# Moving the first load of V's diagonal block to SyncE's queue, and two GpSimd steps to later rounds, in a causal attention + PReLU MLP kernel

## The chip, the cores and the metric

One NeuronCore of one Trainium2 chip runs the whole program. The metric is device time in microseconds (us) of one execution; lower is better. The engines are TensorE (PE), VectorE (DVE), ScalarE (ACT), GpSimd (POOL) and SyncE (SP). SP only issues DMAs here; ACT and POOL issue a few as well. Each engine runs its instructions strictly in the order in which they are written, and waits on semaphores for the others.

## The reference, cut to what matters

```python
# q, k, v: (4, 12, 448, 64) float32; w_in (768, 2048); w_out (2048, 768); alpha (2048,)
scores = q @ k.transpose(0, 1, 3, 2) / sqrt(64)
scores = where(upper triangle, -1e9, scores)
attn = softmax(scores)                     # with the row maximum taken off
x = (attn @ v).transpose(0, 2, 1, 3).reshape(1792, 768)
h = x @ w_in
g = maximum(h, 0) + alpha * minimum(h, 0)
return g @ w_out                           # (1792, 768)
```

## The kernel before

**Tiles.** Attention works on 24 pairs of heads, p = 0 to 23 (four batches, six pairs each). A row of 448 positions is cut into a first piece of 64 and three blocks of 128. For each pair the scores of block i are built in a PSUM bank (`scores`, L563 and L555), DVE masks them and takes the row maximum (`row_max`, L576), ACT takes the exponential and the row sums (`row_exp`, L591), DVE forms the reciprocals (`row_rec`, L604 and L605), POOL multiplies (`row_norm`, L534), PE transposes (`transpose_p`, L642; `transpose_halves`, L633), ACT or DVE copies the transposes out of PSUM (`pt_copy`, L530 on ACT, L532 on DVE), and PE multiplies by V (`av`, L661; `av_halves`, L669). The last of these, L669, reads the 64-row diagonal blocks of V from `vd`, four tiles used in turn (`vd[p % 4]`), which `load_vd` fills by two DMAs a pair (L504). POOL clears the four tiles once at the start (L495).

**MLP.** Both matrix products that follow (L408 and L1342) use a seven-product block scheme: sums and differences of blocks, each split into a rounded high part (`x1h`) and a remainder (`x1l`). While attention runs, spare slots on the engines already prepare its operands: `t_hi` rounds a block on POOL (the letter `h`, a TENSOR_SCALAR on L534 that writes `x1h`), `t_lo` takes the remainder on DVE (the letter `l`, L737), `t_four` forms a difference of two blocks on POOL (the digit `4`, L752), and the first weights are decoded from raw words by `A`, `I`, `C`, `D`, `G` and `+` (`+` is an integer addition on POOL, L331; `C` is a clamp on POOL, L315; `D` is a shift on DVE, L319) and by `S`, `sub`, `pcast` and `cast` (`sub` is L390 on POOL).

**What sets the order.** Attention is written round by round. In round n a string of step names with lags says what is emitted: `EX10+2` means the exponential of block 1, first head, of pair n - 2. `ORDER` is the string of most rounds; `ROUNDS` gives rounds 2 and 3, and the dictionary `first` gives changed strings to some rounds. Instructions are emitted in that order, so it is the order on each engine. Steps in short: `LK`, `LQ` load K and Q (lag 0), `S0`, `S1`, `S2` are scores, `MX` maxima, `EX` exponentials, `RC` reciprocals, `NO` the multiplications, `PT` and `PTH` transposes, `C10`, `C00`, `C20`, `C21`, `C30` the copies out of PSUM (`a` on ACT, `d` on DVE), `AV` and `AH` the products with V, `LW` is `load_vd`. The table `EARLY` says for each round which preparing steps are put into it: `l`, `D`, `G`, `S` run in the middle of the round ahead of the reciprocals, `h`, `4`, `+`, `sub`, `pcast`, `C` after the POOL multiplications of that round. On PE a round begins with `PTH`, `AV`, `AH` of pair n - 4, then `PT` of pair n - 3 (12 matmuls on L642), then scores of pair n - 1.

**Queues.** K, Q and most of V come through SP's queue, K of pairs 0 and 1 through ACT's and part of V through POOL's. `load_vd` uses ACT's queue for pair 0 and SP's for the others. For pair 0 it stands in round 1, behind `LQ+0`; that is ahead of the first exponentials in ACT's order.

Of the kernel before, what the change touches and what calls it, by code (L numbers as in the profile page):

```python
# [24 lines left out]
WARM = 8  # L25
EARLY = {
# [4 lines left out]
}  # L31
GAP = {25: "l", 26: "l"}
# [8 lines left out]
ORDER = """  # L41
# [2 lines left out]
ROUNDS = {2: """  # L44
LK+0 LQ+0 EX10+2 EX11+2 MX00+2 EX00+2 MX01+2 EX01+2 MX20+2 EX20+2 MX21+2 EX21+2 RA+2 NO10+2p NO11+2p NO00+2p NO01+2p MX30+2 S0+1 S1+1 PT1+2 PT0+2 MX10+1 MX11+1 EX30+2 RB+2 NO20+2p NO21+2d NO30+2p
""", 3: """
LK+0 LQ+0 EX10+2 EX11+2 MX00+2 EX00+2 MX01+2 EX01+2 MX20+2 S2+2 EX20+2 MX21+2 PT2+3 EX21+2 C00+3d C20+3a C21+3d C10+3d S0+1 S1+1 SF+1 LW+2 MX30+2 EX30+2 RC+2 NO10+2p NO11+2p NO00+2p NO01+2p NO20+2p NO21+2p NO30+2p MX10+1 MX11+1
"""}


# [143 lines left out]
def kernel(  # L194
# [10 lines left out]
    nc = tc.nc  # L205
    B, NPAIR, D, _, S = qt.shape
# [4 lines left out]
    LQ = S - NQ * QP  # L211
# [249 lines left out]
    T, vs, p3, masks, qd, vd = {}, [], [], [], [], []  # L461

    def half(j):
        return slice(j * D, (j + 1) * D)
# [32 lines left out]
    def load_vd(p):  # L497

        b, hp = pairs[p]
        for j in range(2):  # L500
            x = v[b, hp, :LQ, j]
            stride = x.ap[0][0]
            x = bass.AP(tensor=x.tensor, offset=x.offset, ap=[list(x.ap[0]), [(QP - CP) * stride + 2 * D, NQ + 1], list(x.ap[-1])])
            (nc.sync if p else nc.scalar).dma_start(out=vd[p % 4][half(j), :, j], in_=x)  # L504

    def load_v(b):
        for hs, n in ((hs, n) for hs in ((slice(0, NK), slice(NK, NPAIR)) if b == 0 else (slice(0, NPAIR),)) for n in range(NQ)):
# [242 lines left out]
    def t_four():  # L750
# [4 lines left out]
        "LV": load_v_next, "RC": row_rec, "RA": lambda p: row_rec(p, slice(0, 4)),  # L755
        "RB": lambda p: row_rec(p, slice(4, 2 * NQ + 1)), "AV": av, "AH": av_halves,
        "PTH": transpose_halves, "LW": load_vd, "BB": lambda p: None, "XH": x_hi, "XF": x_sums, "XL": x_lo,
        "ST": lambda p: flush(stores), "XN": lambda p: None, "LT": lambda p: None,
    }
# [25 lines left out]
    def order_of(text):  # L785
        order = []
        for w in text.split():
            name, lag = w.split("+")
            if name in choice:
                eng = {"a": nc.scalar, "d": nc.vector, "p": nc.gpsimd}[lag[-1]]  # L790
                order.append((int(lag[:-1]), name, lambda p, fn=choice[name], eng=eng: fn(p, eng)))
            else:
                order.append((int(lag), name, steps[name]))
        return order

    def attention(hooks):
        order, first = order_of(ORDER), {n: order_of(x) for n, x in ROUNDS.items()}

        for n in (5, 6, 7, 11, 12, 13, 20, 21, 22, 23):
            text = ORDER.replace("C00+3a", "C00+3d") if n in (5, 6, 11, 20, 22) else ORDER  # L800
            if n in (6, 7, 11, 12, 13, 21, 23):
                text = text.replace("C30+4a ", "").replace("MX20+2 ", "MX20+2 C30+4d ")
            first[n] = order_of(text)
        first[1], first[4] = order_of(ORDER.replace("LW+1 ", "").replace("LQ+0", "LQ+0 LW+1")), order_of(ORDER.replace("C00+3a", "C00+3d").replace("LW+1", "LW+2 LW+1"))

        text = ORDER.replace("C10+3a ", "").replace("EH+4 ", "EH+4 C10+3a ").replace("PT2+3 ", "PT2+3 PTH+3 ")
        first[26] = order_of(text.replace("C21+3d ", "C21+3d C30+3d "))
        first[27] = order_of(ORDER.replace("PTH+4 ", "").replace("C30+4a ", ""))
        last = max(lag for lag, *_ in order)
        for n in range(len(pairs) + last):  # L810
            for lag, name, fn in first.get(n, order):
                if 0 <= n - lag < len(pairs):
                    fn(n - lag)
                    for hook in hooks.get((n - lag, name), ()):
                        hook()
# [61 lines left out]
    def ready_bank():  # L877

        b = ring.popleft()
        nc.tensor.matmul(b[:, :S], wi[0, "A11"][:, 0, :P], x1h[:, 0, 0], start=True, stop=True, skip_group_check=True)  # L880
        return b
# [66 lines left out]
    with tc.manual_schedule():  # L948
# [15 lines left out]
        for t in masks:  # L964
# [5 lines left out]
            out=mk, in_=mk, pattern=[[-1, QP]], compare_op=ALU.is_ge, fill=NEG, base=0,  # L970
# [22 lines left out]
        after(last, "LT", scores_over)  # L993
        after(last, "AH", attention_over)
        attention(hooks)
        t13, t24 = (tf[:, 2 * i : 2 * i + 2].rearrange("p a k n -> p (a k n)") for i in range(2))
        rooms["t"], rooms["v"] = Slots([]), Slots([])
# [6 lines left out]
        v_, z, y, x = ring.popleft(), ready_bank(), ring.popleft(), ring.popleft()  # L1004
# [544 lines left out]
```

## Time and profile before

| What | Value |
|---|---|
| Three runs, median (lowest to highest) | 584.0 us (583.35 to 584.0) |
| The profiled execution: time, and span from first to last instruction | 583.36 us, 581.6 us |
| PE busy | 568.9 us, 98% |
| DVE busy | 471.4 us, 81% |
| ACT busy | 384.8 us, 66% |
| POOL busy | 290.1 us, 50% |
| Mean granted TensorE clock | 0.990 of full |
| Attention | from the start to about 175 us of the span |

The page divides the span into 40 slices of 14.5 us. PE is busy for nine tenths or more in nearly all of them; the first slice has six tenths. The row of the granted clock shows full speed everywhere but in the second slice, at six tenths. A busy PE is not a PE at its peak, so a stage is read by what its engines wait for and by the length of its rounds.

### The profile page before, as it was taken

To read this page: it belongs to the slowest core of one execution; us is meant where nothing else is said; L and a number is where in the kernel's file an instruction comes from. 1 tells how busy PE (TensorE), PEld (TensorE's weight loads), DVE (VectorE), ACT (ScalarE), POOL (GpSimd) and SP (SyncE) were. 2 spreads that over 40 slices of the span, in tenths; PEclk is the share of its full clock that TensorE was granted. 3 is DMA by queue.
4 is the path that set the end of the run, shared out by engine and by line. 5 is a ranking of instruction groups with operands and counts; after the bars stand their busy time and mean duration, and the time that the engine had idled before them with its cause. 6 is when DMAs were issued, how large, how long until landed. Compare 5 with 4: busy or idle time off the path is not lost.

```text
span 581.6 us, 11540 instructions
## 1 busy us (share of the span) xinstructions
PE 568.9 (98%) x3921; PEld 503.6 (87%) x3921; DVE 471.4 (81%) x989; ACT 384.8 (66%) x904; POOL 290.1 (50%) x338
## 2 busy tenths in 40 slices
PE   6999999999999999999999999999989999999997
PEld 3577767677788999999999999999989999999997
DVE  1789899999978886768777687888997899797763
ACT  2789888898858565655566655696765666665431
POOL 4666677797753444434454431436144543356420
PEclk9699999999999999999999999999999999999999
DMA  7565654854326675847677657593352414512532
GB/s 186 147 165 120 167 148 105 226 140 130 107 71 227 225 226 201 270 185 243 218 217 257 218 192 230 171 351 127 100 154 80 139 51 133 143 38 91 182 109 108
DMA packets 94074, 95.92 MB, mean 165 GB/s; under 512 B 24096, under 2 KB 83136, under 8 KB 94016
## 3 DMA queue, kind: packets, MB, share of 16 engines
q1 hardware_dynamic: 92624, 93.52, 52.6%
q0 software_dynamic: 528, 1.08, 0.8%
q10 hardware_dynamic: 864, 0.59, 0.4%
q8 instruction: 31, 0.51, 0.4%
q14 instruction: 27, 0.22, 0.1%
HBM read 66.85 MB, written 28.31 MB: 164 GB/s over the span
## 4 chain that ended last, share of the span: by engine, by line
PE 84%; DVE 9%; ACT 2%; DMA 2%; issue 1%; POOL 1%; ACTq 0%; SPq 0%; DVEq 0%; POOLq 0%
PE bank L408 36%; PE bank L1342 32%; PE bank L563 5%; PE bank L642 4%; PE bank L661 3%; DVE bank L576 2%; PE bank L633 2%; PE bank L669 1%; ACT p L591 1%; DVE tf L693 1%; POOL p L534 1%; DMA v<-in_v_dram 1%; DVE x1l L737 1%; DMA kr<-in_k_dram 1%; DVE ptf L532 1%
## 5 line engine op out<-in xcount | busy, mean ns | idle before, releaser
L534 POOL TENSOR_SCALAR p<-p,rs 128x320 f32<-128x320 f32 (+3 forms) x165 | 83.6, 526 | 45.0 <-DVE rs L605 24.5
L1342 PE MATMUL bank<-x1h,x1l 128*128 128x384 f32 x540 | 98.7, 335 | 1.0 <-DVE x1h L1279 0.9
L1342 PEld LDWEIGHTS bank<-x1h,x1l 128*128 128x128 f32 x540 | 94.3, 188 | 1.6 <-DVE x1h L1279 1.2
L591 ACT ACTIVATE p<-bank,nm 128x192 f32<-128x192 f32 (+3 forms) x168 | 81.6, 510 | 21.0 <-DVE nm L576 13.5
L576 DVE CUSTOM_DVE_ANT_0 bank<-bank,mask 128x192 f32<-128x192 f32 (+3 forms) x168 | 70.4, 483 | 12.1 <-PE bank L563 6.1
L432 ACT ACTIVATE tf<-bank 128x448 f32<-128x448 f32 x64 | 34.3, 541 | 40.1 <-PE bank L408 30.1
L563 PE MATMUL bank<-kr,qr 64*128 64x448 f32 (+2 forms) x288 | 55.5, 476 | 5.0 <-ACT p L591 4.7
L436 DVE SCALAR_TENSOR_TENSOR tf<-tf,om,bank 128x448 f32<-128x448 f32 x64 | 41.6, 674 | 6.4 <-ACT tf L432 6.0
L408 PE MATMUL bank<-x1h,wir 128*128 128x448 f32 x192 | 44.7, 368 | 0.0
L563 PEld LDWEIGHTS bank<-kr,qr 64*128 64x128 f32 x288 | 30.3, 198 | 16.4 <-ACT p L591 9.4
L1342 PE MATMUL bank<-x1h,gset 128*128 128x384 f32 x216 | 40.4, 338 | 0.9 <-DVE acc L1355 0.9
L1342 PEld LDWEIGHTS bank<-x1h,gset 128*128 128x128 f32 x216 | 37.9, 188 | 1.2 <-ACT acc L1476 1.2
L642 PE MATMUL bank<-ident,p 128*128 128x128 f32 x288 | 38.5, 284 | 0.3 <-POOL p L534 0.2
L408 PEld LDWEIGHTS bank<-x1h,wir 128*128 128x128 f32 x192 | 35.9, 188 | 3.4
L591 ACT ACTIVATION_READ_ACCUMULATOR p<-bank,nm 128x1 f32 x168 | 36.8, 219 | 0.0
L331 POOL TENSOR_TENSOR dec<-dec,tf 128x768 int32<-128x768 int32 x11 | 22.1, 2009 | 29.1 <-ACT tf L432 15.6
L1320 POOL TENSOR_TENSOR x1l<-acc,x1l 128x512 fp32r<-128x512 f32 x12 | 16.3, 1362 | 40.7 <-ACT x1l L1316 31.7
L530 ACT ACTIVATE ptf<-bank 128x256 f32<-128x256 f32 (+2 forms) x80 | 34.7, 501 | 2.9 <-PE bank L642 1.6
L422 DVE TENSOR_TENSOR bank<-bank,tf 128x448 f32<-128x448 f32 x30 | 18.9, 629 | 20.7 <-PE bank L408 19.4
L642 PEld LDWEIGHTS bank<-ident,p 128*128 128x128 f32 x288 | 31.9, 143 | 4.0 <-POOL p L534 2.2
L661 PE MATMUL bank<-ptf,v 128*64 128x128 f32 (+2 forms) x288 | 35.3, 380 | 0.0
L408 PE MATMUL bank<-x1h,wie 128*128 128x448 f32 x144 | 33.4, 367 | 0.0
(196 smaller groups left out, 1398.3 us busy)
## 6 DMA issues: line engine op xcount, KB each, us to landing
gd<-tf SPq DMA_DIRECT2D x64, 224.0 KB, 2.0
tf<-gd SPq DMA_DIRECT2D x28, 256.0 KB, 4.5
acc<-gd SPq DMA_DIRECT2D x28, 256.0 KB, 4.3
dec<-in_moe_w_in_dram SPq DMA_DIRECT2D x9, 768.0 KB, 5.2
tf<-in_moe_w_in_dram SPq DMA_DIRECT2D x7, 768.0 KB, 4.6
dec<-in_moe_w_out_dram SPq DMA_DIRECT2D x7, 768.0 KB, 4.9
tf<-in_moe_w_out_dram SPq DMA_DIRECT2D x7, 768.0 KB, 4.2
dec<-wd SPq DMA_DIRECT2D x13, 384.0 KB, 4.9
```

Of the source, the lines that this page charges most:

```text
L331: nc.gpsimd.tensor_tensor(out=y, in0=y, in1=low, op=ALU.add)
L408: nc.tensor.matmul(ps, w[:, u, k * P : (k + 1) * P], x[:, k], start=(st in ("P1", "P5") and i == 0), stop=(i == len(mms) - 1), skip_group_ ...
L432: nc.scalar.activation(t, bank_of(g, b, role), AF.Relu, scale=-1.0)
L436: stt(out=t, in0=t, scalar=om[:, f : f + 1], in1=bank_of(g, b, role), op0=ALU.mult, op1=ALU.add)
L530: eng.activation(out, x, AF.Copy, scale=side)
L534: eng.tensor_scalar(out=out, in0=x, scalar1=side, scalar2=1.0, op0=ALU.mult, op1=ALU.mult)
L563: nc.tensor.matmul(ps[:, o : o + lim], T["q", p][half(j), i * QP : (i + 1) * QP], T["k", p][half(j), :lim], start=(o == 0), stop=(n > 0 or ...
L576: nc.vector.tensor_tensor_reduce(out=t, in0=t, in1=mask_of(i), scale=-SCALE, scalar=MOST_F32, op0=ALU.add, op1=ALU.min, accum_out=nm,)
L591: nc.scalar.activation(T["p", p, i][:, j, : t.shape[1]], t, AF.Exp, scale=-1.0, bias=T.pop(("nm", p, i, j)), accum_out=T["sm", p][:, z : z ...
L642: nc.tensor.transpose(ps[:, j - js[0], c], t[:, j, c * QP : (c + 1) * QP], T["ident"])
L661: nc.tensor.matmul(out[half(j), c * QP + LQ :], vs[b % 2][:, hp, c, j], x[:, : (NQ - c) * QP], start=(c == 0), stop=False, skip_group_chec ...
L1342: nc.tensor.matmul(ps, x, w, start=(st in ("P1", "P5")[: 1 if Q else 2] and i == 0), stop=(i == len(mms) - 1), skip_group_check=True,)
```

## The change

There are three parts in the diff.

1. `load_vd` always issues on SP, and the load of pair 0 is written in round 3, as `LW+3` ahead of `LW+2`, no longer in round 1.
2. In `EARLY`, round 15 loses `4 h`, round 18 gets a `4`, round 24 gets an `h`. The steps come from iterators, so the second `4` runs in round 16 and the third in round 18, and each `h` from the fourth on runs one round later.
3. Round 13 leaves the list of rounds in which `C30` (the copy of the 64-row transposes of pair n - 4) goes to DVE, so that there it stays on ACT, as in `ORDER`.

```diff
-    14: "G:1:0 +:1:0 h 4", 15: "G:1:1 +:1:1 4 h", 16: "l l 4 h", 17: "S:S1 h pcast:A11", 18: "S:S2 l h sub:A11 pcast:S1",
-    19: "l sub:S1 h pcast:S2", 20: "l sub:S2 h A:2", 21: "l h C:2", 22: "l h I:2", 23: "l h", 24: "S:S3 l",
+    14: "G:1:0 +:1:0 h 4", 15: "G:1:1 +:1:1", 16: "l l 4 h", 17: "S:S1 h pcast:A11", 18: "S:S2 l h 4 sub:A11 pcast:S1",
+    19: "l sub:S1 h pcast:S2", 20: "l sub:S2 h A:2", 21: "l h C:2", 22: "l h I:2", 23: "l h", 24: "S:S3 l h",
...
-            (nc.sync if p else nc.scalar).dma_start(out=vd[p % 4][half(j), :, j], in_=x)
+            nc.sync.dma_start(out=vd[p % 4][half(j), :, j], in_=x)
...
-            if n in (6, 7, 11, 12, 13, 21, 23):
+            if n in (6, 7, 11, 12, 21, 23):
...
-        first[1], first[4] = order_of(ORDER.replace("LW+1 ", "").replace("LQ+0", "LQ+0 LW+1")), ...
+        first[1], first[4] = order_of(ORDER.replace("LW+1 ", "")), ...
```

In the string of round 3, `... S0+1 S1+1 SF+1 LW+2 MX30+2 ...` becomes `... S0+1 S1+1 SF+1 LW+3 LW+2 MX30+2 ...`.

ACT's queue at the start, before (`mask` are the causal masks, `vd_171` is the tile of pair 0, `p_1` the exponentials of block 1, `bank` a PSUM bank, `nm` the row maximum):

```order
L973 ACT_TABLE_LOAD
L973 ACTIVATE mask_147<-tf 128x128
L976 ACTIVATE mask_148<-tf 64x64 x2
L504 DMA vd_171<-in_v_dram 64x4x64 x2
L591 ACTIVATE p_1_208,sm_209<-bank_62,nm_1_0_196 128x320
L591 ACTIVATE p_1_208,sm_209<-bank_63,nm_1_1_198 128x320
```

The same place in the changed kernel:

```order
L973 ACT_TABLE_LOAD
L973 ACTIVATE mask_147<-tf 128x128
L976 ACTIVATE mask_148<-tf 64x64 x2
L591 ACTIVATE p_1_206,sm_207<-bank_62,nm_1_0_194 128x320
L591 ACTIVATE p_1_206,sm_207<-bank_63,nm_1_1_196 128x320
```

The two DMAs that stood between the masks and the first exponential are gone from ACT.

SP's queue in rounds 2 to 4 (`kr`, `qr` and `qd` are K, Q and the first 64 columns of Q; `vd_173` is the tile of pair 1; rows marked - and + that differ only in a number are the same loads):

```order
 L512 DMA v_167<-in_v_dram 48x3x128
-L473 DMA kr_257<-in_k_dram 64x448 x2
-L473 DMA qr_260<-in_q_dram 64x384 x2
-L477 DMA qd_102<-in_q_dram 64x3x64 x2
+L473 DMA kr_255<-in_k_dram 64x448 x2
+L473 DMA qr_258<-in_q_dram 64x384 x2
+L477 DMA qd_102<-in_q_dram 64x3x64 x2
+L504 DMA vd_171<-in_v_dram 64x4x64 x2
 L504 DMA vd_173<-in_v_dram 64x4x64 x2
 L473 DMA kr_325<-in_k_dram 64x448 x2
```

The load of pair 0 now stands behind K and Q of round 3, ahead of pair 1's block and of K of pair 4.

POOL from the last addition `+` of round 15 to round 18, before (the rows that write `p` are the multiplications of one pair; `rs` the reciprocals):

```order
L331 TENSOR_TENSOR dec<-dec 128x3x128
L752 TENSOR_TENSOR tf<-tf 128x448
L534 TENSOR_SCALAR x1h<-tf 128x448
L534 TENSOR_SCALAR p_1_1512<-p_1_1512,rs_1565 128x320 x2
```

and, with round 18's row group, in the changed kernel:

```order
L331 TENSOR_TENSOR dec<-dec 128x3x128
L534 TENSOR_SCALAR p_1_1510<-p_1_1510,rs_1563 128x320 x2
...
L534 TENSOR_SCALAR x1h<-tf 128x448
L752 TENSOR_TENSOR tf<-tf 128x448
L390 TENSOR_TENSOR wie<-dec,wie 128x384
L534 TENSOR_SCALAR wie<-dec 128x384
```

Round 15 ends with the addition alone, and in round 18 the third difference stands between the rounding and the remainder of A11.

## Rows read from the trace of the kernel before

**Rows 1.** Busy time by stretch: stretch, length, busy and count by engine, clock, DMA.

```profile
14.00:15.00 1.00, 0.24 (x1) 0.24 (x2) 0.92 (x5) 1.00 (x5) 0.00 (x0) 0.50 0.67 148
24.00:25.00 1.00, 1.00 (x24) 0.79 (x24) 0.74 (x3) 0.73 (x4) 1.00 (x3) 0.89 0.98 198
```

**Rows 2.** Timeline of ACT: start, length, instruction, count, idle before and its releaser.

```profile
11.72 1.32 ACTq L504 DMA_DIRECT2D vd<-in_v_dram  x2
13.09 0.53 ACT L591 ACTIVATE p<-bank,nm 128x320 f32<-128x320 f32 x1 [7.20 <-DMA kr<-in_k_dram]
...
25.02 0.39 ACT L530 ACTIVATE ptf<-bank 128x256 f32<-128x256 f32 x1 [0.29 <-PE bank L555]
```

**Rows 3.** The chain that ended last, in order of time, first 20 us.

```profile
6.95 4.69 DMA v<-in_v_dram
```

**Rows 4.** Timeline of DVE, first 21 us.

```profile
7.37 0.14 DVE L576 DVE_READ_ACCUMULATOR2_ANT nm<- 128x1 f32 x1
...
13.74 0.37 DVE L576 CUSTOM_DVE_ANT_0 bank<-bank,mask 128x192 f32<-128x192 f32 x1 [5.77 <-ACT p L591]
...
20.83 1.15 DVE L532 COPY ptf<-bank 128x384 f32<-128x384 f32 x2 [0.72 <-PE bank L642]
```

**Rows 5.** Timeline of PE, the first wait and the starts of five rounds' transposes.

```profile
14.76 1.86 PE L563 MATMUL bank<-kr,qr 64*128 64x448 f32 x2 [4.72 <-ACT p L591]
...
26.66 1.53 PE L642 MATMUL bank<-ident,p 128*128 128x128 f32 x12
...
75.54 1.53 PE L642 MATMUL bank<-ident,p 128*128 128x128 f32 x12
...
100.67 1.53 PE L642 MATMUL bank<-ident,p 128*128 128x128 f32 x12
...
107.18 1.53 PE L642 MATMUL bank<-ident,p 128*128 128x128 f32 x12
...
112.95 1.53 PE L642 MATMUL bank<-ident,p 128*128 128x128 f32 x12
```

**Rows 6.** Timeline of POOL and SP at the start, and landing times of `vd`.

```profile
12.17 1.25 SPq L504 DMA_DIRECT2D vd<-in_v_dram  x2
...
16.26 2.96 POOL L534 TENSOR_SCALAR p<-p,rs 128x320 f32<-128x320 f32 x6 [8.31 <-DVE nm L576]
...
DMA to landing us min/median/max: 2.4/3.2/4.2
```

**Rows 7.** Timeline of POOL and DVE, end of round 15 and start of round 16.

```profile
100.16 1.01 POOL L331 TENSOR_TENSOR dec<-dec 128x384 int32<-128x384 int32 x1
101.14 1.13 POOL L752 TENSOR_TENSOR tf<-tf 128x448 f32<-128x448 f32 x1
102.26 0.55 POOL L534 TENSOR_SCALAR x1h<-tf 128x448 fp32r<-128x448 f32 x1
...
100.39 2.90 DVE L737 TENSOR_TENSOR x1l<-tf,x1h 128x448 fp32r<-128x448 f32 x1
```

**Rows 8.** Timeline of POOL, DVE, ACT and PE, rounds 18 to 21.

```profile
119.81 1.00 POOL L390 TENSOR_TENSOR wie<-dec,wie 128x384 fp32r<-128x384 f32 x1
...
118.51 0.62 DVE L737 TENSOR_TENSOR x1l<-tf,x1h 128x448 fp32r<-128x448 f32 x1
...
120.09 0.75 DVE L604 TENSOR_TENSOR sm<-sm,least 128x7 f32<-128x7 f32 x1 [0.42 <-ACT p L591]
...
130.37 2.02 DVE L737 TENSOR_TENSOR x1l<-tf,x1h 128x448 fp32r<-128x448 f32 x1
...
123.14 0.38 ACT L530 ACTIVATE ptf<-bank 128x256 f32<-128x256 f32 x1
...
123.92 0.63 PE L669 MATMUL bank<-ptf,vd 128*64 128x64 f32 x16
```

**Rows 9.** Timeline of DVE and ACT in round 13.

```profile
81.77 0.56 DVE L319 TENSOR_SCALAR dec<-dec 128x768 int32<-128x768 int32 x1 [0.21 <-POOL dec L315]
...
83.49 0.54 ACT L530 ACTIVATE x1h<-bank 128x448 fp32r<-128x448 f32 x1 [0.80 <-DVE sm L604]
```

More of the change, by code (lines that the diff above doesn't have):

```diff
@@ L46 @@
 """, 3: """
-LK+0 LQ+0 EX10+2 EX11+2 MX00+2 EX00+2 MX01+2 EX01+2 MX20+2 S2+2 EX20+2 MX21+2 PT2+3 EX21+2 C00+3d C20+3a C21+3d C10+3d S0+1 S1+1 SF+1 LW+2 MX30+2 EX30+2 RC+2 NO10+2p NO11+2p NO00+2p NO01+2p NO20+2p NO21+2p NO30+2p MX10+1 MX11+1
+LK+0 LQ+0 EX10+2 EX11+2 MX00+2 EX00+2 MX01+2 EX01+2 MX20+2 S2+2 EX20+2 MX21+2 PT2+3 EX21+2 C00+3d C20+3a C21+3d C10+3d S0+1 S1+1 SF+1 LW+3 LW+2 MX30+2 EX30+2 RC+2 NO10+2p NO11+2p NO00+2p NO01+2p NO20+2p NO21+2p NO30+2p MX10+1 MX11+1
 """}
@@ L800, in attention @@
             text = ORDER.replace("C00+3a", "C00+3d") if n in (5, 6, 11, 20, 22) else ORDER
-            if n in (6, 7, 11, 12, 13, 21, 23):
+            if n in (6, 7, 11, 12, 21, 23):
                 text = text.replace("C30+4a ", "").replace("MX20+2 ", "MX20+2 C30+4d ")
             first[n] = order_of(text)
-        first[1], first[4] = order_of(ORDER.replace("LW+1 ", "").replace("LQ+0", "LQ+0 LW+1")), order_of(ORDER.replace("C00+3a", "C00+3d").replace("LW+1", "LW+2 LW+1"))
+        first[1], first[4] = order_of(ORDER.replace("LW+1 ", "")), order_of(ORDER.replace("C00+3a", "C00+3d").replace("LW+1", "LW+2 LW+1"))
         text = ORDER.replace("C10+3a ", "").replace("EH+4 ", "EH+4 C10+3a ").replace("PT2+3 ", "PT2+3 PTH+3 ")
```

## The prediction, made blind

> **What bounds the kernel now.** I read the page's slices first. PE is busy nearly throughout, so a saving counts only where PE itself waits, or where it works slowly. The second slice is the one with a lower granted clock. I split it by the microsecond: the clock is 0.50 (1.2 GHz) in the stretch from 14 us and back at 0.89, on its way to 2.4 GHz, in the stretch from 24 us [rows 1]. So some 10 us run at half speed. Then I looked for what PE did before the clock fell: PE waited 4.72 us, until 14.76, for an exponential on ACT [rows 5]. DVE waited 5.77 us for the same ACT line [rows 4] and POOL 8.31 us, until 16.26, for DVE [rows 6]. So at the start everybody waits for ACT. The timeline of ACT shows why: its first exponential starts at 13.09 after 7.20 us of idleness, and right before it stand two DMA issues on ACT's own queue, 11.72 to 13.04 [rows 2]. The trace names a K load as the releaser of the exponential. The chain of waits is the better witness: it goes from a V load that takes from 6.95 to 11.64 straight into those issues [rows 3]. They are the loads of V's first diagonal block. ACT cannot pass them, and they cannot be issued before the earlier load has landed. From about 26 us on, rounds are regular. They take 6.11 us on average over the eight from 26.66 to 75.54; where PE waits for nothing a round takes 5.77 (107.18 to 112.95) [rows 5].
>
> **Part 1: the load leaves ACT.** The change removes two issues, 1.32 us, and the wait in front of them. What the first exponential then needs is its row maximum, which is read out at 7.37 and takes 0.14 [rows 4]: it can start at 7.55 and not at 13.09. That is 5.54 us for ACT. Lined up behind it are DVE's next maxima (they share a bank with it), PE's last scores of pair 1, POOL's multiplications and PE's first transposes; each was waiting for the one ahead [rows 4 to 6], so each moves by the same 5.54. What is late next? PE's last scores may start by 9.2, while PE, whose earlier work ends at 10.04, is still busy: no wait is left there. POOL starts at 10.72, and PE's first transposes half a microsecond later. The longest hole in PE is then under 1 us, against 4.72.
>
> Beside it stands the clock. It fell some 4 us after PE had stopped. I take it that without that hole it stays at 2.4 GHz: a choice, since no row shows PE with holes of this smaller size. Then two waits for a slow PE go too: DVE's 0.72 for the transposes at 20.83 [rows 4] and ACT's 0.29 at 25.02 [rows 2]. The sum is 5.54 + 0.72 + 0.29 = 6.55 us. The bounds are 5.54, or somewhat less, with the clock falling again (first rival), and 6.55.
>
> A rule speaks against a gain of this size. The Trainium skill (DMA: Bandwidth & Descriptors, section Issuing engines are not separate DMA queues) says that DMAs from all engines end up on the same 16 DMA engines, and that the choice of issuer only saves the sequencer's time to initiate them. By that the saving would be the 1.32 us of the two issues, and the sum 583.36 - 1.32 = 582.0. The trace disagrees as far as ACT's 7.20 us go: the queue's wait costs more than the issue.
>
> The two issues now stand on SP, where pair 1's block was issued at 12.17 in 1.25 us [rows 6]. The new load takes that place, pair 1's goes to 13.4, and K of pair 4 behind them to 14.7 or later. The block lands at most 4.2 us after its issue [rows 6], by 17.6. Its reader, the products at the end of the round before 26.66 (0.63 us on the row at 123.92 [rows 8], so from 26.0), moves to about 19.5: 2 us to spare. K of pair 4 is first read a round after 26.66, at some 26 us when shifted. Both cost nothing. If the first cover were gone, each microsecond of lateness would be one for PE.
>
> Does it carry to the end? From 26 us on the rounds wait for one another's engines and not for the clock on the wall, and the page's chain runs through PE to the end; loads of weights wait for room that the same engines free. So I let the 6.55 stand in full.
>
> **Part 2: POOL's steps.** In round 15 the order on POOL was the addition 1.01, the difference 1.13, the rounding 0.55, until 102.81. DVE's remainder L737 took 2.90 us from 100.39 on [rows 7], against 0.62 elsewhere [rows 8]: it came through only when POOL was through. With the addition alone it should end near 101.8, not 103.29, 1.5 us earlier. What that is worth is seen on PE: the round from 100.67 to 107.18 took 6.51, 0.74 over the 5.77 of an undisturbed one [rows 5]. So -0.74, bounds 0 and -0.74; I take the whole, as the next round shows that PE can do it.
>
> The Trainium skill (SBUF — State Buffer, section SBUF: two separate sides) says that DVE and GpSimd share a port pair as an exclusive lock held for a whole instruction. By that alone DVE would have got in between the addition and the difference, the removal would bring nothing, and the sum would be 0.74 us higher. The 2.90 us speak against it here.
>
> In round 18 the third difference now stands ahead of the remainder of A11, at 119.81 [rows 8]. DVE's reciprocal step L604 came at 120.09 and took 0.75, until that POOL instruction ended; with 1.13 more in front it ends near 121.95. The chain behind it is: maxima, exponentials, then ACT's copy at 123.14 (0.38), which PE's products at 123.92 need [rows 8]. Moved by 1.13 the copy ends at 124.5 or so, and PE waits some 0.6. Bounds 0 (DVE may come earlier after the saving in round 15) and 0.6. I take 0.5, near the event of round 15, which cost 0.74 for 1.68 us of POOL. In round 21 the remainder L737 takes 2.02, 1.40 over its 0.62 [rows 8]; POOL's order there comes 1.1 later, so that the clash may vanish or grow. I take 0, with -1 to +0.7. Round 24's rounding falls where POOL has nothing else to do: 0. Sum -0.24, bounds -1.7 and +1.3.
>
> **Part 3: the copy of round 13.** DVE loses about 0.4 us, ACT gets it (0.38 on the row of 123.14 [rows 8]). DVE waits there for POOL's clamp anyway (0.21 us, at 81.77), and ACT idles 0.80 before 83.49 [rows 9]. Cost 0; without that cover 0.4.
>
> **The sum.** 6.55 + 0.24 = 6.8 us, from 583.36 to 576.6. The profiled execution lies 0.64 below the median of the three runs and at their lowest; I put the new median halfway, at 576.9.
>
> **The rivals.**
> *The clock falls all the same.* For: between 10.5 and 14 us PE would do little but transposes in POOL's pace. Against: no hole of 4 us is left. Then only 5.54 is gained at the start, and the 10 us at half speed now lie 5.5 us deep over rounds that ran at full speed before, so that PE falls about 2.7 us behind. The eight rounds up to 75.54 are 6.11 - 5.77 = 0.34 longer than PE needs, which is 2.7 to catch up with. So 4.5 to 5.5 remain, say 5.2: 583.36 - 5.2 - 0.2 = 578.0, with up to 579.4.
>
> *POOL's order costs more than it gives.* Rounds 18 to 21 lose their full 1.3: 583.36 - 6.55 + 1.3 - 0.74 = 577.4, or 578.1 if round 15 gives nothing.
>
> *The change does not do what it says:* the first exponential finds another wait, and only the 1.32 us of issues go. For: the trace names a K load as releaser. Against: the exponential stands behind nothing but its maximum in the new order. 582.0.
>
> *The slower side: the diagonal block comes late.* It now is issued behind K, Q and V loads on SP. It decides if it lands after 26.0, when its reader runs now: then PE waits there and the start's gain is gone; landing at 28 would give 583.36 + 2.0 = 585.4. Against it stands 17.6 worked out above; 8.4 us would have to go wrong.
>
> **How the numbers follow.** About 0.2% (1.2 us) is what a measurement of this kernel can tell from no change. Forecast 0.60 (575.2 to 577.6), clock falls 0.22, POOL's order 0.09, only the issues saved 0.05, block late 0.04. Faster: the first three and nearly all that 582.0 holds, 0.93; same 0.03; slower 0.04. The range goes from 575.2 (the sum with POOL's better bound, 583.36 - 6.55 - 1.7, rounded up) to 579.4, the upper end of the clock rival; what lies outside is the last two and a little more, within 2 in 10. The median is 576.9.
>
> **What would show it.** Right: ACT's first exponential near 7.6, no wait of microseconds on PE before 16, a granted clock of 1.00 in all slices, and the transposes that started at 26.66 starting near 20. Round 15 to 16: L737 at 1.4 or less, PE's round at 5.8. Wrong: 0.50 in the windows from 14 us on (first rival), a wait of L669 for a DMA (late block), L604 over 1.5 us in round 19 with PE waiting behind it. If the start of regular rounds moves by 6 us and the end by less, the loss lies in rounds 13 to 24, and my claim that the shift carries through is the step that failed.

## The result and the profile after

The changed kernel takes 576.62 us in the median (575.5 to 577.26, four executions) beside 584.0 us for the kernel before on the same chip: a ratio of 0.987 with a 95% interval of 0.9847 to 0.9892, or 7.4 us less. The prediction was 576.9.

The profiled execution took 575.5 us with a span of 573.7, so 7.9 us less than that of before. First the page of the kernel after, its span and two rows of the 40 slices:

```profile
span 573.7 us, 11533 instructions
...
PE   8999999999999999999999999999989999999997
...
PEclk9999999999999999999999999999999999999999
```

The second slice, six tenths before, is at full speed. By stretches, in the columns of [rows 1] (the clock is the third number from the end):

```profile
14.00:15.00 1.00, 1.00 (x10) 0.88 (x10) 1.00 (x4) 0.90 (x3) 1.00 (x3) 1.00 0.78 202
24.00:25.00 1.00, 1.00 (x20) 0.74 (x18) 1.00 (x7) 1.00 (x5) 0.86 (x2) 1.00 0.88 324
```

The timelines of the kernel after at the start, of ACT, DVE, PE and SP (start, length, instruction, idle before and its releaser):

```profile
6.97 0.53 ACT L591 ACTIVATE p<-bank,nm 128x320 f32<-128x320 f32 x1 [1.69 <-DVE nm L576]
...
17.71 0.38 ACT L530 ACTIVATE ptf<-bank 128x256 f32<-128x256 f32 x1
```

```profile
7.62 0.37 DVE L576 CUSTOM_DVE_ANT_0 bank<-bank,mask 128x192 f32<-128x192 f32 x1 [0.24 <-ACT p L591]
...
13.58 1.48 DVE L532 COPY ptf<-bank 128x256 f32<-128x256 f32 x3
```

```profile
10.74 1.24 PE L642 MATMUL bank<-ident,p 128*128 128x128 f32 x5 [1.08 <-POOL p L534]
...
18.14 0.69 PE L669 MATMUL bank<-ptf,vd 128*64 128x64 f32 x16 [0.28 <-ACT ptf L530]
```

```profile
12.17 2.62 SPq L504 DMA_DIRECT2D vd<-in_v_dram  x4
```

The first exponential starts at 6.97 and not at 13.09 [rows 2], and now waits for its row maximum on DVE. PE's longest hole is 1.08 us and not 4.72 [rows 5]. The two waits for a slow PE are gone: DVE copies at 13.58 without the 0.72 of [rows 4], ACT at 17.71 without the 0.29 of [rows 2]. SP issues both diagonal blocks in one go from 12.17, and the products that read the first (18.14) wait only for ACT's copy, no DMA.

Where the 7.9 us lie is best seen from the starts of PE's twelve transposes on L642, one group a round, before and after:

| Start before | Start after | Gained so far |
|---|---|---|
| 26.66 | 18.76 | 7.90 |
| 32.90 | 25.32 | 7.58 |
| 94.30 | 86.66 | 7.64 |
| 100.67 | 93.03 | 7.64 |
| 107.18 | 98.80 | 8.38 |
| 124.49 | 116.11 | 8.38 |
| 130.26 | 122.30 | 7.96 |
| 137.00 | 129.12 | 7.88 |
| 166.08 | 158.21 | 7.87 |
| span 581.6 | 573.7 | 7.9 |

All but some 0.3 us is gained ahead of 33 us (7.58) and carried through to the end. The step of 0.74 between 93.03 and 98.80 is the second part, in full; 0.50 of it is lost again between 116 and 129 us. POOL and DVE in the round from 93.03 and in the later ones:

```profile
92.53 1.01 POOL L331 TENSOR_TENSOR dec<-dec 128x384 int32<-128x384 int32 x1
...
110.48 1.51 POOL L752 TENSOR_TENSOR tf<-tf 128x448 f32<-128x448 f32 x1
111.95 0.99 POOL L390 TENSOR_TENSOR wie<-dec,wie 128x384 fp32r<-128x384 f32 x1
...
117.19 0.99 POOL L390 TENSOR_TENSOR wie<-dec,wie 128x384 fp32r<-128x384 f32 x1
...
122.51 1.00 POOL L390 TENSOR_TENSOR wie<-dec,wie 128x384 fp32r<-128x384 f32 x1
123.49 0.56 POOL L534 TENSOR_SCALAR x1h<-tf 128x448 fp32r<-128x448 f32 x1
```

```profile
92.75 1.81 DVE L737 TENSOR_TENSOR x1l<-tf,x1h 128x448 fp32r<-128x448 f32 x2
...
111.62 0.40 DVE L604 TENSOR_TENSOR sm<-sm,least 128x7 f32<-128x7 f32 x1
...
117.39 0.82 DVE L604 TENSOR_TENSOR sm<-sm,least 128x7 f32<-128x7 f32 x1 [0.42 <-ACT p L591]
122.42 2.10 DVE L737 TENSOR_TENSOR x1l<-tf,x1h 128x448 fp32r<-128x448 f32 x1
```

In the round of 93.03 the addition stands alone on POOL, and two remainders L737 on DVE take 1.81 us together, beside 2.90 for the first alone in [rows 7]. In round 18 the moved difference (110.48) stands ahead of the remainder at 111.95, and DVE's L604 (111.62) ends with the difference, at 112.02: it came in between the two POOL instructions. A round later the remainder on L390 starts 1.08 us after PE's transposes (117.19 against 116.11), where it started 0.59 after them in the kernel before (125.08 against 124.49). It now lies on L604 (117.39, until 118.21), and PE's round from 116.11 takes 6.19 and not 5.77.

### The profile page after: what moved, and what is told of

It reads as the page before. It is cut to its first block, busy times and chain, and to the rows that moved or that the text cites. A ratio compares the mean times of both kernels' runs of the same rounds, so it can differ in the third digit from the quotient of the medians.

```text
span 573.7 us, 11533 instructions
## 1 busy us (share of the span) xinstructions
PE 564.8 (98%) x3921; PEld 501.2 (87%) x3921; DVE 470.9 (82%) x988; ACT 386.0 (67%) x905; POOL 289.2 (50%) x338
## 3 DMA queue, kind: packets, MB, share of 16 engines
q0 software_dynamic: 528, 1.08, 0.7%
## 4 chain that ended last, share of the span: by engine, by line
PE 88%; DVE 7%; ACT 2%; issue 1%; POOL 1%; DVEq 0%; ACTq 0%; POOLq 0%
PE bank L408 36%; PE bank L1342 33%; PE bank L563 6%; PE bank L642 5%; PE bank L661 4%; PE bank L633 2%; ACT p L591 2%; PE bank L669 2%; DVE bank L576 1%; PE bank L458 1%; DVE tf L693 1%; DVE ptf L532 1%; DVE x1l L1320 1%; POOL p L534 1%; DVE x1h L1279 0%
## 5 line engine op out<-in xcount | busy, mean ns | idle before, releaser
L576 DVE CUSTOM_DVE_ANT_0 bank<-bank,mask 128x192 f32<-128x192 f32 (+3 forms) x168 | 70.5, 487 | 7.0 <-PE bank L563 6.6
L563 PE MATMUL bank<-kr,qr 64*128 64x320 f32 (+2 forms) x288 | 52.8, 451 | 0.3 <-issue 0.2
L563 PEld LDWEIGHTS bank<-kr,qr 64*128 64x128 f32 x288 | 29.1, 186 | 11.4 <-ACT p L591 3.7
L642 PE MATMUL bank<-ident,p 128*128 128x128 f32 x288 | 37.5, 278 | 1.4 <-POOL p L534 1.3
L530 ACT ACTIVATE ptf<-bank 128x512 f32<-128x512 f32 (+2 forms) x81 | 35.0, 496 | 2.6 <-PE bank L642 1.6
L642 PEld LDWEIGHTS bank<-ident,p 128*128 128x128 f32 x288 | 31.1, 140 | 4.5 <-POOL p L534 2.9
```

The source lines that it names most:

```text
L530: eng.activation(out, x, AF.Copy, scale=side)
L563: nc.tensor.matmul(ps[:, o : o + lim], T["q", p][half(j), i * QP : (i + 1) * QP], T["k", p][half(j), :lim], start=(o == 0), stop=(n > 0 or ...
L576: nc.vector.tensor_tensor_reduce(out=t, in0=t, in1=mask_of(i), scale=-SCALE, scalar=MOST_F32, op0=ALU.add, op1=ALU.min, accum_out=nm,)
L642: nc.tensor.transpose(ps[:, j - js[0], c], t[:, j, c * QP : (c + 1) * QP], T["ident"])
```

## The experiments

Ten kernels, each beside the kernel before on its chip. First the medians; the profiles stand below. A ratio weighs every execution, so it is not exactly the quotient of the two medians; savings given with an interval are worked out from the ratio.

| Kernel | Median, us | Ratio to before (95%) | First exponential | L642 of the first regular round | From the one to the other | Clock below 1.00 in |
|---|---|---|---|---|---|---|
| before | 584.0 | | 13.09 | 26.66 | 13.57 | 14 to 25 |
| after | 576.62 | 0.987 (0.9847 to 0.9892) | 6.97 | 18.76 | 11.79 | none |
| e1_load_only | 577.81 | 0.9904 (0.9884 to 0.9925) | 7.15 | 19.62 | 12.47 | 12 to 17 |
| e2_order_only | 582.88 | 0.9987 (0.9978 to 0.9997) | 12.71 | 26.62 | 13.91 | 10 to 25 |
| e3_act_round3 | 576.87 | 0.9882 (0.9869 to 0.9895) | 7.00 | 20.33 | 13.33 | 12 to 16 |
| e4_sync_round1 | 576.48 | 0.9879 (0.9864 to 0.9893) | 7.06 | 18.84 | 11.78 | none |
| e5_before_busy | 584.04 | 0.9998 (0.9989 to 1.0007) | 12.97 | 26.45 | 13.48 | 16 to 24 |
| e6_after_busy | 575.73 | 0.9858 (0.9845 to 0.9871) | 7.19 | 18.97 | 11.78 | none |
| e7_diff_round24 | 576.23 | 0.9866 (0.985 to 0.9882) | 7.44 | 20.00 | 12.56 | 13 to 17 |
| e8_copy_vector | 576.65 | 0.989 (0.9869 to 0.9911) | 6.91 | 18.69 | 11.78 | none |
| e9_other_slot | 583.38 | 0.999 (0.9979 to 1.0) | 12.71 | 26.67 | 13.96 | 11 to 25 |
| e10_before_no_hole | 583.36 | 0.9993 (0.9983 to 1.0003) | 13.48 | 26.21 | 12.73 | 20 to 24 |

The four right columns are from the one profiled execution of each. The medians of before in the comparisons were 583.93 (e1 to e4), 583.99 (e5 to e8) and 583.63 (e9, e10).

**Each part alone.** The first experiment takes only the load's move:

```diff
-LK+0 ... S0+1 S1+1 SF+1 LW+2 MX30+2 ...
+LK+0 ... S0+1 S1+1 SF+1 LW+3 LW+2 MX30+2 ...
-            (nc.sync if p else nc.scalar).dma_start(...)
+            nc.sync.dma_start(...)
...
-first[1], ... = order_of(ORDER.replace("LW+1 ", "").replace("LQ+0", "LQ+0 LW+1")), ...
+first[1], ... = order_of(ORDER.replace("LW+1 ", "")), ...
```

> The kernel before with the first part alone: the first diagonal block of V goes to SyncE's queue, behind K and Q of round 3; GpSimd's order and the copy of round 13 stay as before. Theory (the first part carries nearly the whole gain, and ScalarE's in-order wait is what it takes away): the first exponential near 7.0 us, a granted clock of 1.00 in all stretches from 8 to 22 us, a saving of 7.6 us against the profiled execution of before (583.36), so 575.7 to 577. Rival 1 (a good part of the gain comes from GpSimd's order): 578 or more. Rival 2 (only the 1.32 us of the two issues are saved): 582.0.

It saves 5.6 us of 584 (4.4 to 6.8 by the interval): by far the larger part, less than the 7.6 that I expected. The windows of this execution show a part of the reason (columns as in [rows 1]):

```profile
12.00:13.00 1.00, 0.73 (x6) 0.43 (x5) 1.00 (x6) 0.54 (x4) 1.00 (x3) 0.84 0.47 113
13.00:14.00 1.00, 1.00 (x8) 0.89 (x5) 1.00 (x5) 1.00 (x5) 1.00 (x4) 0.50 0.30 67
...
16.00:17.00 1.00, 1.00 (x10) 0.47 (x6) 0.49 (x5) 0.41 (x2) 0.00 (x0) 0.95 0.94 161
```

```profile
10.93 1.25 PE L642 MATMUL bank<-ident,p 128*128 128x128 f32 x5 [1.09 <-POOL p L534]
```

The clock still falls to 0.50 (1.2 GHz), for some three microseconds and not ten, about two after PE's hole of 1.09 us. My expectation "1.00 in all stretches" was wrong for this execution. All four executions of e1 had a mean clock between 0.994 and 0.997; of the four of the kernel after two had 0.997 (576.86 and 577.26) and two 1.000 (575.5 and 576.39).

The second takes only the order of POOL and the copy:

```diff
-14: "G:1:0 +:1:0 h 4", 15: "G:1:1 +:1:1 4 h", ... 18: "S:S2 l h sub:A11 pcast:S1", ... 24: "S:S3 l",
+14: "G:1:0 +:1:0 h 4", 15: "G:1:1 +:1:1", ... 18: "S:S2 l h 4 sub:A11 pcast:S1", ... 24: "S:S3 l h",
-            if n in (6, 7, 11, 12, 13, 21, 23):
+            if n in (6, 7, 11, 12, 21, 23):
```

> The kernel before with the second and third part alone: one difference of GpSimd from round 15 to 18, its rounding from round 21 to 24, the copy of round 13 on ScalarE; the load of V stays on ScalarE's queue in round 1. Theory: 0.74 us gained between rounds 15 and 16, 0.4 to 0.5 lost near round 20, 0.1 lost at round 21, so 0.2 us less than before, which a measurement can't tell from none: 583.1 to 584. Rival (with the later start gone, the steps meet others and the whole gain of 0.74 stays, or is lost): 582.6 or 584.4.

It saves 0.76 us (0.2 to 1.3), more than the 0.2 that I expected: the median of 582.88 lies below the range that I named for the theory, nearer the rival's 582.6. With e1 it adds up to 6.4, against 7.6 (6.3 to 8.9) measured for both together by the ratio; the intervals overlap.

**Queue or place?** The third puts the load back on ACT's queue, in its new place; the fourth puts it on SP's queue, in its old place.

```diff
e3, against after:
-            nc.sync.dma_start(...)
+            (nc.sync if p else nc.scalar).dma_start(...)
e4, against after:
-first[1], ... = order_of(ORDER.replace("LW+1 ", "")), ...
+first[1], ... = order_of(ORDER.replace("LW+1 ", "").replace("LQ+0", "LQ+0 LW+1")), ...
```

In e4 `LW+3` goes from round 3 as well.

> The kernel after with the load of the first diagonal block on ScalarE's queue again, but in round 3, where SyncE has it: the place is the new one, the queue the old one. Theory (the wait for an earlier load, ahead of the first exponential, was the cost, and not the queue as such): the first exponential stays near 7.0 us and the time rises by the two issues at most, 1.3 us, if they stand in front of an exponential that somebody waits for: 575.5 to 577.9. Rival (ScalarE's queue is the wrong one in every place): 579 or more, with a wait of several us on ScalarE in round 3.

> The kernel after with the load on SyncE's queue, but in round 1, behind the first Q and K as it was on ScalarE: the queue is the new one, the place the old one. Theory (only who waits matters): SyncE waits there until the earlier load of V has landed, near 11.6 us, and issues then; the exponential is free near 7.0 us; K of the next pairs comes later by the wait, which has some us of cover: 575.5 to 577.5. Rival (the place matters: the wait on SyncE holds the following loads of K and Q back, and PE waits for them in rounds 2 to 5): 578 to 582.

Both give the whole gain. So neither the queue nor the place costs anything measurable by itself. ACT of e3 and SP of e4:

```profile
14.07 0.66 ACTq L504 DMA_DIRECT2D vd<-in_v_dram  x1
...
15.17 0.64 ACTq L504 DMA_DIRECT2D vd<-in_v_dram  x1
16.10 0.32 ACT L591 ACTIVATE p<-bank,nm 128x64 f32<-128x64 f32 x1 [1.17 <-DVE nm L576]
```

```profile
4.31 1.71 SPq L504 DMA_DIRECT2D vd<-in_v_dram  x2
```

In e3 the two issues take 1.30 us of ACT's time beside its exponentials and its median is 0.25 us over after, within the noise. The surprise is e4: I expected SP to wait until 11.6 us there, and it issued the block at 4.31. So nothing in the data made the block wait for the V load of [rows 3]. What did is in the built program. There each load of SP and ACT takes one of eight completion semaphores in turn, and is not issued before the load that had the semaphore last has landed. These are the waits of the block and of the loads beside it in the kernel before, and of the block in e4 (`DMAHW0` to `DMAHW7` are the eight):

```
before, ACT: L504 DMA vd0_171<-in_v_dram 64x4x64 [waits DMAHW5_49,Pool_49]
before, ACT: L504 DMA vd0_171<-in_v_dram 64x4x64 [waits DMAHW7_49]
before, SP:  L512 DMA v0_167<-in_v_dram 80x3x128 [waits DMAHW5_49]
before, SP:  L473 DMA kr_3_257<-in_k_dram 64x448 [waits DMAHW7_49,PE_49]
e4, SP:      L504 DMA vd0_171<-in_v_dram 64x4x64 [waits DMAHW1_49,Pool_49]
```

On ACT's queue the block's first issue was given the semaphore that the V load issued at 6.95 had, its second that of the first half of K of pair 3; on SP's, in the same round, the first issue got one whose load had landed before SP came to it. A further run tests it.

**The semaphore.** Here the two V loads that SP issues near 7 us go to POOL's queue, and the semaphores shift by two: the block's two issues now follow the first halves of Q of pair 2 and of K of pair 3.

```diff
-(nc.gpsimd if b == 0 and (n < 2 or hs.start) else nc.sync).dma_start(
+(nc.gpsimd if b == 0 else nc.sync).dma_start(
```

> The kernel before with the two loads of V that SyncE issues near 7 us (line 512, rows of the third block) put on GpSimd's queue, where the other four are. The diagonal block stays on ScalarE's queue ahead of the first exponential. In the built program each load of SyncE and ScalarE takes one of eight completion semaphores in turn and waits until the load that had it before has landed; by the move the two issues of the block wait for the first halves of Q of pair 2 and of K of pair 3 and no longer for a load of V. Theory (ScalarE's wait is for whichever load had the semaphore before): the second issue starts within 0.1 us of the landing of K of pair 3's first half, issued near 7 us, so near 10.5 to 11; the first exponential near 11.3 to 11.8 and not 13.0; all later rounds 1.2 to 1.8 us earlier: 582.2 to 582.8 in the median. Rival (the wait is for V's own memory or for the transfers' bandwidth, not for the semaphore): the first exponential stays at 12.7 to 13.1, 583.5 to 584.3.

The chain of waits of e2 (as before) and of e9, in order of time:

```profile
7.00 4.23 DMA v<-in_v_dram
11.23 0.02 issue
11.26 0.02 ACTq L504
11.27 0.04 issue
11.31 0.66 ACTq L504
```

```profile
7.35 4.67 DMA kr<-in_k_dram
12.02 0.02 issue
12.04 0.62 ACTq L504
12.66 0.05 issue
12.71 0.53 ACT p L591
```

The wait moved exactly as the semaphores say: in e2 the issue comes 0.08 us after V's landing, in e9 the second issue 0.02 us after K's. V has no part in it: its two moved loads landed at 12.6 and 13.2 in e9, after that issue. That settles what ACT waited for. The gain did not come: K landed after 4.67 us and not after 3.6 or so, at 12.02, so the first exponential started at 12.71, and the time fell by 0.6 us (0 to 1.2 by the interval), not by the 1.2 to 1.8 expected. By these two numbers alone the rival would do as well; it is the moment of the issue that decides. There was little to gain: in the kernel before, the block's second issue had the same half of K to wait for, which landed near 12.1 there.

**The clock.** Two kernels keep PE busy in the kernel before with matrix multiplications that nobody needs, one does so in the kernel after (the edit of e10; e5 and e6 put a fixed number in one place):

```diff
+for _ in range(FILL.get((p, i), 0)):
+    nc.tensor.matmul(banks[0], warm_sb[:, :P], warm_sb, start=True, stop=True)
 for j, ps in enumerate(banks):
     nc.tensor.matmul(ps[:, o : o + lim], ...
```

> The kernel before with 18 matrix multiplications of 512 columns more on TensorE, ahead of the scores of pair 1, into a bank that those scores then overwrite; nobody reads what they make. The load stays on ScalarE's queue, so the first exponential still starts near 13 us; only TensorE's hole of 4.72 us shrinks to about 1 us. Theory (a part of the saving is the clock): no 0.50 in the windows from 14 to 24 us, the wait of VectorE at 20.8 and of ScalarE at 25.0 vanish, the regular rounds start about 1.0 to 1.5 us earlier: 582.4 to 583.0 in the median. Rival 1 (the clock's fall costs nothing that stays, the engines behind ScalarE set the pace): 583.6 to 584.4. Rival 2 (the clock falls though TensorE is busy): 0.50 in the windows, 584 or more.

> The kernel before with 25 matrix multiplications of 512 columns more on TensorE: 21 ahead of the scores of pair 1, 4 ahead of its last scores, each into a bank that the scores then overwrite; nobody reads what they make. The load stays on ScalarE's queue and the first exponential near 13 us; TensorE's holes up to 17 us shrink to 0.3 us or less. Theory (what the first part saves beyond the first exponential's 6.1 us is the clock): granted clock 1.00 in all windows to 26 us, the transposes of the first regular round start 11.8 us after the first exponential, as in the kernel after, so near 24.8 and not 26.6, and 1.5 us of that stay: 582.4 in the median. Rival (other waits hold the rounds, the clock is worth nothing): transposes at 26.4 or later, 583.6 to 584.2.

> The kernel after with 4 matrix multiplications of 512 columns more on TensorE, ahead of the last scores of pair 1, into a bank that those overwrite, so that TensorE's longest hole at the start shrinks from 1.08 us to about 0.2. Theory (the hole of 1.08 us is what lets the clock fall in some executions, to a mean of 0.997, and each such fall costs 0.9 us or so): every execution at a mean clock of 1.00, none above 576.5, median 575.5 to 576.2. Rival (the fall in these executions has another cause, or the executions differ for other reasons): clocks of 0.997 remain, median 576.4 to 577.

PE of e5, and the windows at the fall; then PE of e10 and its windows:

```profile
14.64 1.02 PE L566 MATMUL bank<-kr,qr 64*128 64x448 f32 x2 [0.79 <-ACT p L594]
16.74 1.99 PE L645 MATMUL bank<-ident,p 128*128 128x128 f32 x6 [1.08 <-POOL p L535]
```

```profile
16.00:17.00 1.00, 0.26 (x2) 0.20 (x2) 1.00 (x7) 1.00 (x5) 0.85 (x2) 0.98 0.00 0
17.00:18.00 1.00, 0.99 (x5) 0.47 (x3) 0.93 (x5) 0.82 (x4) 1.00 (x3) 0.50 0.00 0
```

```profile
17.25 1.25 PE L645 MATMUL bank<-ident,p 128*128 128x128 f32 x5 [1.08 <-POOL p L535]
```

```profile
19.00:20.00 1.00, 0.98 (x11) 0.82 (x10) 1.00 (x5) 1.00 (x5) 1.00 (x3) 1.00 0.00 0
20.00:21.00 1.00, 1.00 (x6) 0.69 (x6) 1.00 (x5) 1.00 (x5) 1.00 (x3) 0.50 0.23 50
```

In both the hole of 4.72 us is filled, and the clock falls all the same, later: after the holes of 0.79 and 1.08 us in e5, after the one of 1.08 us in e10, where PE waits for POOL as in the kernel after. My fillers did not reach that hole, since the four in e10 ran before 14.6 us, ahead of the last scores, and the hole is behind those. So neither run shows the kernel before at full clock, and neither median moves (e5 not at all, e10 by 0.4, -0.2 to 1.0). As tests of the clock's price they are inconclusive. Within e10, three executions had a mean clock of 1.000 (581.86, 582.06, 583.8) and two of 0.993 (583.67, 584.63): the right direction, with much scatter.

In e6 the fillers do reach the hole:

```profile
10.96 1.25 PE L645 MATMUL bank<-ident,p 128*128 128x128 f32 x5 [0.22 <-POOL p L535]
12.47 0.33 PE L645 MATMUL bank<-ident,p 128*128 128x128 f32 x1 [0.27 <-POOL p L535]
```

All four executions have a mean clock of 0.999 or 1.000, from 575.12 to 576.25, and the median is 575.73. That is as expected: the hole of 1.08 us is what lets the clock fall in half the executions of the kernel after. Of the 26 executions of the six kernels with that hole (after, e1, e3, e4, e7, e8), 19 have a mean clock of 0.997 or less. It is also the best median of all kernels here, 0.9 us under after; as the intervals overlap, a gain over the changed kernel is likely but not shown.

The clock's price is read from the table. From the first exponential to the transposes of the first regular round the work is the same in all kernels (e3 has two issues in it). It takes 11.78 or 11.79 us in the four profiles without a fall, 12.47 to 12.73 where the fall lasts some three microseconds (e1, e7, e10), and 13.48 to 13.96 where it lasts longer (before, e2, e5, e9). A long fall thus costs 1.7 to 2.2 us at that point, a short one 0.7 to 0.9. That is not yet the price at the end. PE of e10, near 70 us:

```profile
68.68 1.53 PE L645 MATMUL bank<-ident,p 128*128 128x128 f32 x12
70.78 2.27 PE L566 MATMUL bank<-kr,qr 64*128 64x320 f32 x12 [0.56 <-DMA qr<-in_q_dram]
...
75.47 1.53 PE L645 MATMUL bank<-ident,p 128*128 128x128 f32 x12
```

In this profile the transposes run 0.45 us ahead of those of before from 26.21 on (26.66 in before) to 68.68 (69.13). The next ones are only 0.07 ahead (75.54 in before), since the scores in between waited for a load of Q: what the shorter fall had saved was lost there, and the span is that of before. In the kernels that start like the changed one the fall does show at the end: of the 18 executions of after, e4, e7 and e8, seven with a mean clock of 0.999 or more have a median of 575.5 us, the eleven others 576.95. These are executions set beside each other, not a test. Two of the eleven, of e8, took 579.0 and 579.5, as one of e1 took 580.35, at mean clocks of 0.996 or 0.997; what made them so long is open.

**The order on POOL.** Two more tell apart what is in the second and third part. In e7 the third difference goes on to round 24, ahead of its rounding; there it comes after the block has been used, so that this kernel computes another operand, with the same work.

```diff
e7, against after:
-18: "S:S2 l h 4 sub:A11 pcast:S1", ... 24: "S:S3 l h",
+18: "S:S2 l h sub:A11 pcast:S1", ... 24: "S:S3 l 4 h",
e8, against after:
-            if n in (6, 7, 11, 12, 21, 23):
+            if n in (6, 7, 11, 12, 13, 21, 23):
```

> The kernel after with GpSimd's third difference moved on from round 18 to round 24, right ahead of its rounding. Theory (in round 18 it pushes the int32 addition of round 19 into VectorE's reciprocal chain, which costs TensorE 0.4 to 0.5 us by round 21): 0.4 to 0.5 us less than after, 576.1 in the median. Rival 1 (what is lost there comes and goes with the alignment of the engines, which differs from execution to execution): no difference from after within 0.3 us. Rival 2 (the difference ahead of its rounding makes the rounding late for its reader): 577 or more.

> The kernel after with the copy of round 13 on VectorE again. Theory (the copy lies beside a wait for GpSimd on either engine): as after, within 0.3 us: 576.3 to 576.9. Rival (it is on the path on VectorE): 0.4 us more, 577.0.

e8 is at 576.65, as after: the copy of round 13 costs nothing measurable on either engine. e7 is 0.4 us under after, as the theory had it, but the intervals do not tell that from none. Its profile speaks against the theory, in which the difference in round 18 makes the later round long: with the difference gone from there, the round of PE that starts at 116.11 in after still takes 6.60 us there (0.83 over 5.77), while in e3 and e4, which have the difference in round 18, it takes 5.77 and a later one 6.4. These rounds trade their waits from execution to execution. Summed up they are steadier. From the transposes that start at 94.30 in before to those three rounds later, the five kernels with the old order (before, e1, e5, e9, e10) take 18.39 to 18.65 us, the seven with the new one 17.90 to 18.19, a gain of 0.2 to 0.75. Over the six rounds behind, the old take 35.80 to 36.08, the new 35.42 to 36.28: as much lost as gained.

## Why the prediction was right, and where it was not

**First exponential (forecast 5.54 earlier): right in mechanism, a little small.** It came 6.12 earlier in the two traces. 0.58 of that was luck of the start: the first row maximum itself came earlier (DVE's L576 at 6.38, not 6.96). Over the table the five kernels with the load on ACT in round 1 start it at 12.71 to 13.48, the seven others at 6.91 to 7.44; the means, 12.99 and 7.10, are 5.9 apart.

**Why ACT waited: right that it did, wrong in what it waited for.** I read from the chain [rows 3] that the block "cannot be issued before the earlier load has landed", which held for this build; but it was the turn of the semaphores, not V's data, as e4 (issue at 4.31) and e9 (wait moved to K) show. The sum did not suffer.

**The rule on queues.** e3 and e4 show that it makes no measurable difference which of the two engines issues: 576.87 on ACT, 576.48 on SP. With that the Trainium skill (DMA: Bandwidth & Descriptors, section Issuing engines are not separate DMA queues) agrees, when it says that the issuer's choice only saves time to initiate. What the 582.0 drawn from it left out was the wait ahead of the issue: the first exponential came 5.9 us later with the load there, and the issues were only 1.32 us of that.

**The clock (forecast 0.72 + 0.29 = 1.01, all or nothing): mis-sized, and the choice was half wrong.** Without a fall the gain is larger: 1.78 at the first regular round (13.57 - 11.79), of which the next round, 6.56 and not 6.24, gives back 0.32. But the step "without that hole it stays at 2.4 GHz" holds in only two of four executions (7 of 26 over the kernels with the same start). I had forecast a longest hole of under 1 us; it is 1.08, and in the other executions it lets the clock fall for some three microseconds, for 0.7 to 0.9 at the first regular round. My first rival thus comes true in half the executions, with a fall of three microseconds and not of the ten from which I worked out its 5.2 us. The two errors have opposite signs, and the median hid them: 1.46 without a fall, about 0.7 with one.

**Round 15 (forecast 0.74): right to the hundredth in the profile.** L737 is no longer held up until POOL's last step, and PE's round takes 5.77. That it is the hundredth is luck: over the profiles it is 0.2 to 0.75 on three rounds, as the old order lost less there in other executions.

**Round 18 (forecast -0.5): the step failed.** I expected L604 to wait for the difference and the remainder together; it came in between the two (0.40 us at 111.62). With that the Trainium skill agrees (SBUF — State Buffer, section SBUF: two separate sides), which says that the port pair shared by DVE and GpSimd is held for one whole instruction. In this trace L737 at 122.42 took 2.10 us and came through only behind two POOL instructions; the sentence leaves open who gets the port next. A loss of 0.42 came a round later in this profile, and was not there in e3 and e4. So the second part is worth 0.76 by e2 and not 0.24, though the interval (0.2 to 1.3) just takes in the forecast. Rounds 21 and 24 and the third part at 0: as forecast (L737 took 2.10 beside 2.02 in [rows 8]; e8).

**Carried through to the end: right for this shift.** 7.6 us of it stand from 33 us to the end. A smaller one need not be carried: the 0.45 of e10 went in one round, to a wait for a load of Q. **The late block: no**, PE never waited for it. That the sum came out within 0.3 us of the median is in part luck: a clock term too small, a fall that I had given 0.22, and an order term too small by some 0.5 balance. The mechanism and the size of the largest term, the exponential, are shown.

## What to carry to other kernels

An engine that computes and also issues DMAs pays for every wait ahead of the issue, and the wait can be for a load that has nothing to do with it: look at which completion semaphore a load was given, and whose landing it stands for. Moving a load by a queue or a round may help only because it changes that turn. When a hole on TensorE is removed, look for the next smaller one: the clock may still fall there, in some executions and not in others.

## What the runs showed of the hardware

The granted clock fell to 0.50 (1.2 GHz) after a hole of PE of about 1.08 us too, not only after one of 4.72. It did so in the profiles of e1, e3, e7 and e10, and in that of e5 behind holes of 0.79 and 1.08 us; in those of after, e4 and e8, with the same hole of about 1.08, it did not. With 0.22 us in its place (e6) the mean clock was 0.999 or more in all four executions. How long it stayed low differed: about three microseconds in e1, e3, e7 and e10, seven in e5, ten in before, up to fourteen in e2 and e9. What decides between a fall and none after the same hole stays open.
